# The first feed-forward product as seven half-size block products, in tiles of 512 tokens, with x' through DRAM

## Chip, cores, metric

One core of a Trainium2 chip. The metric is the time of one execution in microseconds (us) on the device. A run's profile has its own span (first to last instruction), some 2 us shorter than the time; sums over parts of a trace are sums of spans.

## The reference

Hash-masked attention (4 batches, 8 heads, 768 positions, head size 64), then a feed-forward block on the 3072 tokens. Only the second half is restructured:

```python
h = x @ w_in                                   # 3072 x 512 times 512 x 2048
sp = np.maximum(h, 0.0) + np.log1p(np.exp(-np.abs(h)))
g = h * erf(sp)
return (g @ w_out).astype(np.float32)          # times 2048 x 512
```

All of it is float32. The kernel computes the softplus with exp and log, and erf with a polynomial of three factors and a tanh.

## The kernel before

Tiles of 256 tokens. One unit is 512 rows of h for one tile; two units make an iteration, and there are 24 iterations. Of PSUM, the matmul accumulator, the kernel allots eight banks: three double ones for h and two single ones for the output.

```python
def hidden(u):                                   # first product of one unit
    ps = big("h_ps")[...]                        # one of three double banks
    for f in range(G):                           # 4
        for kc in range(NK):                     # 4
            nc.tensor.matmul(out=ps[:, f, :],    # 128 x 256
                lhsT=w_in_sb[:, kc, ...], rhs=xT[b][:, kc, t0 : t0 + T],
                start=(kc == 0), stop=(kc == NK - 1))
...
for p in range(NP + 3):
    if p < NP:
        hidden(2 * p); hidden(2 * p + 1)
    ...                                          # elementwise work of rounds p-1, p-2, p-3
    if check and 1 <= p:                         # input bounds, in the first 16 iterations
        for m in range(4 * p - 4, 4 * p):
            if m < 2 * B * H:
                extremes(m)                      # a DMA load, then a VectorE reduction
    if p >= 3:
        project(p - 3, 0); project(p - 3, 1)     # second product of round p-3
```

So the iterations 0 to 2 hold first products alone, and three rounds at the end hold second products alone. I call them start and tail, and the 21 in between full iterations.

## Time and profile before

| part of the trace before | from, to (us) | length |
|---|---|---|
| attention | 0 to 372.1 | 372.1 |
| start (iterations 0 to 2) | 372.1 to 414.8 | 42.7 |
| 21 full iterations | 414.8 to 993.6 | 578.8 |
| tail | 993.6 to 1043.4 | 49.8 |

The median time was 1046.42 us (three runs). The table is cut from the chain of work in order of time, whose lines the prediction shows.

### The profile page before, as it was taken

What the parts mean: (1) busy time and instruction counts of PE and PEld (TensorE: products, weight loads), DVE (VectorE), ACT (ScalarE), POOL (GpSimd) and SP (SyncE); (2) the same over time, 40 slices, a digit from 0 to 9 for tenths busy, and PEclk for the clock granted to TensorE, in tenths of its full rate; (3) what the DMA queues carried; (4) which work ended last, traced back from release to release, by engine and by line L of the source; (5) the groups of instructions that cost most, each with busy time, mean ns of one, the idle gap of its engine ahead of it and who ended that gap; (6) DMA issues with size and microseconds to landing.
All of it is one profiled execution on the core that took longest, in us unless ns stands there. A gap on an engine that the chain in (4) does not pass through costs nothing.

```text
span 1043.4 us, 11778 instructions
## 1 busy us (share of the span) xinstructions
PE 1028.2 (99%) x4482; PEld 603.4 (58%) x4482; DVE 797.4 (76%) x983; ACT 674.5 (65%) x770; POOL 16.2 (2%) x34
## 2 busy tenths in 40 slices
PE   7999999999999999999999999999999999999997
PEld 3444444444444478666666666666666666666643
DVE  4788888788888849988878787878786859494981
ACT  4666666565666637887777666666666667585880
POOL 0000000000000000000000000000000000000000
PEclk9999999999999999999999999999999999999999
DMA  8344445444443102011111101110111000000000
GB/s 197 87 102 122 113 134 138 106 102 103 123 123 96 58 17 61 30 35 63 40 41 31 36 30 52 31 51 30 51 31 35 1 21 0 21 1 11 10 21 24
DMA packets 55153, 61.98 MB, mean 59 GB/s; under 512 B 33552, under 2 KB 41744, under 8 KB 55088
## 3 DMA queue, kind: packets, MB, share of 16 engines
q1 hardware_dynamic: 50480, 45.41, 17.0%
q0 software_dynamic: 4320, 15.73, 4.7%
q8 instruction: 37, 0.61, 0.2%
q14 instruction: 28, 0.23, 0.1%
q10 hardware_dynamic: 288, 0.01, 0.0%
HBM read 54.63 MB, written 6.49 MB: 59 GB/s over the span
## 4 chain that ended last, share of the span: by engine, by line
PE 98%; DMA 1%; SPq 0%; DVE 0%; ACT 0%; issue 0%
PE h_ps L594 32%; PE o_ps L672 32%; PE st L319 15%; PE av L356 13%; PE bits L193 4%; PE z_ps L369 2%; DMA q<-in_qkT_dram 1%; SPq L178 0%; DVE ob L681 0%; DVE h L661 0%; SPq L183 0%; SPq L244 0%; ACT qb L209 0%; PE bound L748 0%
## 5 line engine op out<-in xcount | busy, mean ns | idle before, releaser
L594 PE MATMUL h_ps<-xT,w_in_sb 128*128 128x256 f32 x1536 | 335.4, 379 | 0.0
L672 PE MATMUL o_ps<-w_out_sb,h 128*128 128x512 f32 x768 | 333.3, 592 | 1.9 <-DVE h L661 1.9
L594 PEld LDWEIGHTS h_ps<-xT,w_in_sb 128*128 128x128 f32 x1536 | 291.6, 190 | 48.9 <-issue 10.0
L672 PEld LDWEIGHTS o_ps<-w_out_sb,h 128*128 128x128 f32 x768 | 145.8, 190 | 177.0 <-issue 172.7
L331 ACT ACTIVATE e<-st 128x768 f32<-128x768 f32 x192 | 141.1, 808 | 27.1 <-PE st L319 27.1
L356 PE MATMUL av<-e,v 128*64 128x385 f32 (+1 forms) x768 | 138.1, 495 | 0.0
L319 PE MATMUL st<-q,k 64*128 64x384 f32 x768 | 134.3, 482 | 0.0
L344 DVE TENSOR_TENSOR sum<-sum,e 128x768 f32<-128x768 f32 x128 | 121.5, 949 | 8.9
L653 DVE SCALAR_TENSOR_TENSOR s<-q,s 128x1024 f32<-128x1024 f32 x96 | 111.0, 1218 | 18.8 <-ACT q L652 18.8
L621 ACT ACTIVATE e<-e 128x1024 f32<-128x1024 f32 x48 | 50.0, 1049 | 96.2 <-DVE e L608 96.2
L652 ACT ACTIVATE q<-z,cq 128x1024 f32<-128x1024 f32 x96 | 102.5, 1137 | 1.3 <-DVE s L635 1.2
L356 PEld LDWEIGHTS av<-e,v 128*64 128x64 f32 x768 | 49.5, 136 | 80.6 <-issue 72.4
L607 ACT COPY h<-h_ps 128x1024 f32<-128x1024 f32 x48 | 47.9, 1000 | 72.9 <-PE h_ps L594 72.9
L319 PEld LDWEIGHTS st<-q,k 64*128 64x128 f32 x768 | 71.4, 187 | 37.8
L681 DVE COPY ob<-o_ps 128x512 f32<-128x512 f32 x24 | 16.4, 688 | 78.3 <-PE o_ps L672 78.3
L625 DVE TENSOR_TENSOR w<-e,w 128x1024 f32<-128x1024 f32 x48 | 58.8, 1225 | 1.7
L635 DVE SCALAR_TENSOR_TENSOR s<-s,w 128x1024 f32<-128x1024 f32 x48 | 58.8, 1225 | 1.6
L632 DVE SCALAR_TENSOR_TENSOR s<-h,s 128x1024 f32<-128x1024 f32 x48 | 58.5, 1218 | 0.0
L694 DVE TENSOR_REDUCE most<-t 128x1 f32<-128x384 f32 x64 | 33.1, 547 | 31.4 <-DMA t<-in_qkT_dram 31.3
L661 DVE TENSOR_TENSOR h<-h,s 128x1024 f32<-128x1024 f32 x48 | 56.4, 1217 | 0.0
L653 DVE SCALAR_TENSOR_TENSOR s<-z,s 128x1024 f32<-128x1024 f32 x48 | 56.4, 1216 | 0.0
L660 ACT ACTIVATE s<-s 128x1024 f32<-128x1024 f32 x48 | 49.6, 1054 | 9.4 <-DVE s L653 7.2
(58 smaller groups left out, 740.9 us busy)
## 6 DMA issues: line engine op xcount, KB each, us to landing
t<-in_qkT_dram SPq DMA_DIRECT2D x64, 192.0 KB
raw<-in_w_out_dram POOLq DMA_DIRECT2D x16, 512.0 KB, 4.2
raw<-in_w_in_dram POOLq DMA_DIRECT2D x14, 512.0 KB, 4.0
q<-in_qkT_dram SPq DMA_DIRECT2D x32, 192.0 KB
k<-in_qkT_dram SPq DMA_DIRECT2D x32, 192.0 KB
v<-in_v_dram SPq DMA_DIRECT2D x32, 192.0 KB
r<-rd SPq DMA_DIRECT2D x32, 192.0 KB
out_dram<-ob SPq DMA_DIRECT2D x24, 256.0 KB
```

Source lines behind the costliest of these rows:

```text
L319: nc.tensor.matmul(out=d["st"][c][:, ab, 0:HS], lhsT=d["k" + src][rows, keys], rhs=d["q" + src][rows, cols], start=(part == 0), stop=(part ...
L331: nc.scalar.activation(out=e[:, :, 0:HS], in_=st[:, :, 0:HS], func=AF.Exp, scale=scale)
L344: nc.vector.tensor_tensor(out=d[key], in0=d[key], in1=e, op=ALU.add)
L356: nc.tensor.matmul(out=d["av"][rows, 0:w], lhsT=d["v"][:, g * GC + c, rows], rhs=e[:, ab, 0:w], start=(g == 0 and c == 0), stop=(g == 1 an ...
L594: nc.tensor.matmul(out=ps[:, f, :], lhsT=w_in_sb[:, kc, (g * G + f) * P : (g * G + f + 1) * P], rhs=xT[b][:, kc, t0 : t0 + T], start=(kc = ...
L625: nc.vector.tensor_tensor(out=w, in0=e, in1=w, op=ALU.subtract)
L632: nc.vector.scalar_tensor_tensor(out=s, in0=h, scalar=0.0, in1=s, op0=ALU.max, op1=ALU.add)
L635: nc.vector.scalar_tensor_tensor(out=s, in0=s, scalar=S_MAX, in1=w, op0=ALU.min, op1=ALU.add)
L652: nc.scalar.activation(out=q, in_=z, func=AF.Square, bias=cq[:, j : j + 1])
L653: nc.vector.scalar_tensor_tensor(out=s, in0=q, scalar=r, in1=s, op0=ALU.add, op1=ALU.mult)
L661: nc.vector.tensor_tensor(out=d["h"], in0=d["h"], in1=s, op=ALU.mult)
L672: nc.tensor.matmul(out=ps, lhsT=st[t * NG + f // G]["h"][:, f % G, tt * P : (tt + 1) * P], rhs=w_out_sb[:, f, :], start=(f == 0), stop=(f ...
```

## The change

The intent is fewer matmuls. Strassen's scheme in its Winograd form does a product of 2 x 2 blocks with seven block products in place of eight, for extra sums of blocks. Weight sums are made once, during attention; sums of x once per tile; the sums of results come from accumulation in PSUM and three additions on VectorE. x' is the normalised output of attention, the x of the reference above.

```diff
-    T = 256
+    T = 512
+    w_sum = const.tile([P, 3, 2, FH], F32, name="w_sum")
+    xs = [dram.tile([JP, P, S], F32, ...) for b in range(B)]      # x' goes out and comes back
...
+            def product(p, name):
+                into, a, b, first, last = dict(
+                    P1=("X", a11, b11, True, False),
+                    P2=("Y", a12, b21, True, True),
+                    P3=("Z", s4, b22, False, True),
+                    P4=("X", a22, t4, False, True),
+                    P5=("Z", s1, t1, True, False),
+                    P6=("X", s2, t2, False, False),
+                    P7=("X", s3, t3, False, False),
+                )[name]                                            # 4 matmuls of 256 columns each
+            def read(p, q):                                        # ScalarE: X -> h
+                nc.scalar.copy(out=d["h"][:, :, q, :], in_=d["X"])
+            def complete(p, q, which):                             # VectorE: h += Y or Z
+                nc.vector.tensor_tensor(out=h, in0=d[which], in1=h, op=ALU.add)
+            def one_more(p, u):                                    # moved from VectorE
+                nc.scalar.activation(out=w, in_=st[p]["e", u], func=AF.Identity, bias=1.0)
...
+                    for name in ("P1", "P2", "P5"): product(p, name)
+                each(saturate, p - 3); each(gate, p - 3)
+                read(p, 0); complete(p, 0, "Y"); product(p, "P6")
+                project(p - 3, 0)
+                each(square, p - 2); each(factor, p - 2, 0)
+                each(absolute, p - 1); each(multiply, p - 2, 0)
+                read(p, 1); product(p, "P7")
+                project(p - 3, 1); project(p - 3, 2)
+                each(exponential, p - 1); each(one_more, p - 1)
+                presum_x(...); extremes(...) x4; check(...)
+                each(lost, p - 1)
+                read(p, 3); complete(p, 3, "Z"); product(p, "P4"); product(p, "P3")
+                each(logarithm, p - 1); each(softplus, p - 1); each(correct, p - 1)
+                each(factor, p - 2, 1); each(multiply, p - 2, 1)
+                each(factor, p - 2, 2); each(multiply, p - 2, 2)
+                read(p, 2); complete(p, 1, "Z")
+                project(p - 3, 3); store(...)
```

(Cut: the conditions for the first and last iterations, and all that only renames pools.) The order of these calls is the order in each engine's queue. X, Y and Z are one bank each, and four banks hold output, so the three double banks for h are gone.

## The prediction

> **What bounds the kernel now.** I read the page first: engine shares, then the chain that ended last, then the costliest groups.
>
> ```profile
> PE 1028.2 (99%) x4482; PEld 603.4 (58%) x4482; DVE 797.4 (76%) x983; ACT 674.5 (65%) x770; POOL 16.2 (2%) x34
> PE 98%; DMA 1%; SPq 0%; DVE 0%; ACT 0%; issue 0%
> L594 PE MATMUL h_ps<-xT,w_in_sb 128*128 128x256 f32 x1536 | 335.4, 379 | 0.0
> L672 PE MATMUL o_ps<-w_out_sb,h 128*128 128x512 f32 x768 | 333.3, 592 | 1.9 <-DVE h L661 1.9
> ```
>
> TensorE is busy all the time and is 98% of the chain: there is nothing but matmuls to save. Each f32 matmul of the program shows as two records (768 calls, 1536 records). The 379 ns is a latency with overlap; 335.4/1536 = 218 ns is the pitch.
>
> The chain in order of time gives the rhythm of the feed-forward part (columns: start us, us, what):
>
> ```profile
> 372.17 14.01 PE h_ps L594 x64
> 386.98 41.64 PE h_ps L594 x192
> 428.62 13.73 PE o_ps L672 x32
> 442.35 13.81 PE h_ps L594 x64
> ...
> 979.89 27.48 PE o_ps L672 x64
> 1009.28 27.75 PE o_ps L672 x64
> ```
>
> One iteration (24 of them) is 13.81 of first product plus 13.73 of second: 27.54 us. It starts with three iterations of first product alone, without a hole but for a 0.8 us divisor matmul: 372.2 to 414.8, 42.6 us. Then 21 full iterations to 993.6, then 49.8 us of tail: second products, a 1.9 us wait, the last copy and store.
>
> The elementwise groups of one shape, from the list by form, price what is added:
>
> ```profile
> L635 DVE SCALAR_TENSOR_TENSOR s<-s,w 128x1024 f32<-128x1024 f32 x48 | 58.8, 1225 | 1.6
> L608 DVE TENSOR_SCALAR e<-h 128x1024 int32<-128x1024 int32 x48 | 32.8, 684 | 27.2 <-ACT h L607 27.2
> L652 ACT ACTIVATE q<-z,cq 128x1024 f32<-128x1024 f32 x96 | 102.5, 1137 | 1.3 <-DVE s L635 1.2
> L694 DVE TENSOR_REDUCE most<-t 128x1 f32<-128x384 f32 x64 | 33.1, 547 | 31.4 <-DMA t<-in_qkT_dram 31.3
> L681 DVE COPY ob<-o_ps 128x512 f32<-128x512 f32 x24 | 16.4, 688 | 78.3 <-PE o_ps L672 78.3
> ```
>
> Last row but one: the check of extremes, four per iteration in the first 16, waits about 1.95 us each time for a DMA, because only two buffers serve four loads. That wait stays.
>
> [...] 13.81/64 = 216 ns per 256-column record, 13.73/32 = 429 ns per 512. So one matmul less saves its full time, and Strassen's smaller blocks lose nothing, since they keep 256 columns and 128 rows. [...] Trace: 1225 against 684 ns for the same 1024 elements. All block sums are two-source, so full price. [...] the trace shows two loads of 1283 ns per iteration, and I expect two. [...]
>
> **The change, part by part.**
> (1) Removed: per 512-token tile 112 block matmuls in place of 128, so 28 calls (56 records) an iteration in place of 64 records: 8 x 0.2158 = 1.73 us, a period of 12.08 + 13.73 = 25.81 us. In all 24 x 1.73 = 41.4 us, 4.0% of the time: the most it can give.
> (2) VectorE per iteration, from start to start when independent: 14 two-source operations of 1024 (gate 2, multiply 6, lost 2, softplus 2, correct 2) at 1.15 = 16.1; absolute 2 x 0.62 = 1.25; four new completions of 512 from PSUM at about 0.68 (the copy row's size) = 2.7; together 20.1. Block sums of x: four of 512 in four iterations, 0.65 each time. Output copies 4 x 0.69 in every fourth iteration. Extremes 4 x 0.52 + 1.95 wait = 4.0 in the first 16. The four copies share two buffers, so the third waits about 2 us for the store of the first. Mean in the first 16: 20.1 + 0.65 + 0.7 + 0.5 + 4.0 = 25.9, of which 2.4 is waiting; the period of TensorE is 25.81. It has no slack on the mean, but a store burst is 4.7 us late in one iteration and worked off in the three after it.
> (3) ScalarE: tanh, exp, log, square, one_more 10 x 1.0, factor 6 x 1.07, four reads of 512 at 0.58 (between 478 ns for 384 and 1000 for 1024), two loads 2.57: 21.3 us of 25.81.
> (4) The new waits. X, Y and Z are one bank each, so P6, P7, P4, P1 each wait for ScalarE to have read X, and P3, P5 for VectorE to have read Z. In a full iteration the projections of 3.43 us lie between them. I laid the three queues side by side: P7 is wanted at 10.3 us and read 1 ends at 7.6; P4 is wanted at 18.9 and read 3 ends at 12.8; P3 at 20.7 and the completion ends at 15.4; P5 of the next iteration at 29.3, completion at 25 to 28. After a store burst the gates end 6.3 us into the next iteration, the projection wants them at 6.9. So almost all is hidden; I put 0.2 us per iteration for near misses, 4 us. Once, in iteration 20, VectorE stands some 11 us at the check's matmul, which lies behind three projections: about 2.8 us of it reach TensorE.
> (5) The start. Iterations 0 to 2 have no projection to lie between reads. Iteration 0: 12.1 of work, divisor 0.8, then waits for the divisor's copy ahead of read 0, for read 1 and read 3: 15.7. Iteration 1: exp and one_more (4 us) stand in ScalarE's queue between read 1 and read 3, so P4 waits 3 us: 16.3. Iteration 2: square, factor, a table load, exp, one_more before read 3, then load, log and four factors before read 2, which P1 of iteration 3 waits for: about 19.3 of ScalarE work plus waits for VectorE, 23. Sum 55.0 against 42.6 before: +12.4 us, where the saving would have been 5.2.
> (6) The tail. Three more rounds of elementwise work follow, at the pace of ScalarE and VectorE, with only 13.73 of second product each. Following tanh, gate, exp, log, softplus, correct, multiply, gates of round 22 end some 20.6 us after the last first product, where before they ended at 15.6; TensorE idles 6 us there, then runs 27.5 to the end, copy and store 6.4: 54.5, [...] against 49.8: +6.
> (7) Weight sums (8 x 1.15) and x' through DRAM lie in the attention part, where TensorE bounds and VectorE has about 4 us free in 25: hidden, +1 for the handover at the end.
>
> Sum: 1046.4 - 21 x 1.73 (36.3) + 12.4 + 6 + 4 + 2.8 + 1 = 1036 us.
>
> **The rivals.**
> A: fully hidden. The reads slip in everywhere and start and tail cost nothing more; only then does the whole 41 us arrive: 1005 us. For it: TensorE's 98% of the chain, and queues with 10% free. Against it: the start has nothing to lie between reads, and the old kernel had three double banks of PSUM for it. With half of the start hidden and no tail loss it is about 1022.
> B: VectorE becomes the bound in the first 16 iterations. By (2) its mean is 25.9; if completions from PSUM cost 0.2 us more each, or each interleaved wait adds 1.5 us, the period there is 27.5 and that gain is gone: 1036 + 13 x 1.7 = 1058. For it: the DMA wait of the extremes, the store burst with two buffers. Against it: much of the 25.9 is waiting that can overlap other waits.
> C: the handshake on single banks. Each of six dependences costs TensorE a semaphore and 0.6 us even in full iterations: 21 x 2 = 42 us, so 1075. Against it: 3.4 to 7 us of other products stand before each dependent one.
>
> **Range and chances.** The sure part is 36 us of steady gain; the losses at the ends come from queue order and are sure in sign, with some 5 us of error each. B in part is the likelier error upwards, A in part downwards. So 1036, with 1022 to 1049 for 8 in 10. Faster by over 2% means under 1025.5: 0.2. Slower by over 2% needs B and C together: 0.05.
>
> **What would show it.** 1344 first-product records in place of 1536, at the same pitch, busy near 294 us. In the chain, mid-run, iterations of 25.8 to 26.0 us and matmuls nearly without pieces of ACT or DVE. Three first iterations of about 55 us with TensorE waiting for the reads (copies out of X) by 3 to 5 us at a time. A tail near 55 us with one hole of some 6 us. VectorE busy above 90% in iterations 3 to 16, about 80% after. Wrong if iterations in the first 16 are 27 us or more (B), if waits for reads or completions recur in every iteration (C), if the three first iterations take under 48 us (A), if table loads exceed two an iteration, or if attention ends more than 3 us later than before.

Where the recorded text is cut (marked), no trace of this case showed what it said. The figures left in the paragraph that opens with a cut are from the old kernel's trace: 216 and 429 ns a record, 1225 ns for a two-source operation (L635) against 684 for a one-source one (L608), table loads of 1283 ns. The recorded sum comes to 1036.3, given as 1036. The +6 of the tail in it held a term for a lower clock after the hole, which is cut; the terms that stand give 54.5 - 49.8 = +4.7 there, and a sum of 1035.0.

## More of the kernel before

The busy time by stretch (columns: stretch, length, then busy us and count for TensorE, weight loads, VectorE, ScalarE, GpSimd, then granted clock, which is TensorE's share of full speed by the trace, DMA share, GB/s) says what room the other engines had:

```profile
414.80:993.60 578.80, 578.80 (x2020) 383.02 (x2019) 452.06 (x479) 407.94 (x394) 0.00 (x0) 1.00 0.09 29
993.60:1043.40 49.80, 41.50 (x97) 17.84 (x95) 24.27 (x23) 20.18 (x20) 0.00 (x0) 0.96 0.06 23
```

In the full iterations TensorE has no hole at all; VectorE is busy 78% and ScalarE 70%.

## The result

The changed kernel is correct and takes 1032.76 us (1031.75 to 1035.13, 4 runs) against 1046.34 (1045.20 to 1048.01, 4 runs). The ratio is 0.9872, 95% interval 0.9851 to 0.9894: 1.3% faster, within 2%. Ratios in this document are the mean time of one kernel's runs over that of the other's in the same rounds, so not quite the ratio of the medians quoted.

The profiled run is the slowest of the four (span 1033.3). First its engine shares and its chain of work that ended last:

```profile
PE 997.1 (96%) x4290; PEld 569.3 (55%) x4290; DVE 828.1 (80%) x1039; ACT 728.0 (70%) x866; POOL 16.2 (2%) x34
PE 88%; DVE 4%; ACT 3%; DMA 2%; issue 1%; SPq 1%; DVEq 0%; ACTq 0%
```

The chain is no longer TensorE alone: 7% of it is VectorE and ScalarE. Where they stand in it shows in the chain in order of time (start us, us, what). A full iteration:

```profile
457.19 1.73 PE X L699 x8
...
464.10 3.43 PE o_ps L811 x8
...
469.26 6.87 PE o_ps L811 x16
...
479.58 3.43 PE o_ps L811 x8
483.01 1.73 PE X L699 x8
```

From X to X it takes 483.01 - 457.19 = 25.82 us, and every piece between is a matmul. The busy time by stretch, for iterations 1 and 2 and for two parts of the full ones:

```profile
391.55:408.96 17.41, 14.46 (x57) 11.39 (x56) 11.38 (x17) 9.20 (x11) 0.00 (x0) 0.90 0.24 70
408.96:430.33 21.37, 14.20 (x58) 11.32 (x56) 18.43 (x22) 18.75 (x21) 0.00 (x0) 0.92 0.23 74
430.33:767.00 336.67, 336.16 (x1145) 217.51 (x1146) 291.42 (x329) 273.22 (x288) 0.00 (x0) 1.00 0.16 50
767.00:973.00 206.00, 203.64 (x698) 131.76 (x697) 161.64 (x173) 166.44 (x176) 0.00 (x0) 1.00 0.05 17
```

TensorE fills 336.16 of 336.67 us in the first part, with VectorE at 87%. In iterations 1 and 2 it has holes and a granted clock of 0.90 and 0.92. TensorE in order of time shows them (in brackets the idle time before and what ended it):

```profile
403.56 2.62 PE L699 MATMUL X<-ts,w_in_sb 128*128 128x256 f32 x8 [2.27 <-ACT h L713]
406.12 3.00 PE L699 MATMUL Z<-x,w_sum 128*128 128x256 f32 x8
408.96 1.89 PE L699 MATMUL X<-x,w_in_sb 128*128 128x256 f32 x8
...
422.38 3.40 PE L699 MATMUL X<-ts,w_in_sb 128*128 128x256 f32 x8 [3.68 <-ACT h L713]
...
430.33 1.99 PE L699 MATMUL X<-x,w_in_sb 128*128 128x256 f32 x8 [2.81 <-ACT h L713]
```

P4 of iterations 1 and 2 and P1 of iteration 3 wait for reads of X (L713), and after two of the holes the products take 2.62 to 3.40 us in place of 1.9. Why the read was late is in ScalarE's queue of iteration 1:

```profile
399.14 2.00 ACT L735 ACTIVATE e<-e 128x1024 f32<-128x1024 f32 x2
401.05 1.99 ACT L739 ACTIVATE w<-e 128x1024 f32<-128x1024 f32 x2
402.94 0.57 ACT L713 COPY h<-X 128x512 f32<-128x512 f32 x1
```

Exp and one_more, 4 us, stand ahead of read 3. The tail, TensorE again:

```profile
977.06 14.00 PE L811 MATMUL o_ps<-w_out_sb,h 128*128 128x512 f32 x32 [0.23 <-DVE h L799]
996.97 30.28 PE L811 MATMUL o_ps<-w_out_sb,h 128*128 128x512 f32 x64 [5.90 <-DVE h L799]
```

A hole of 5.90 us for the gates (L799), then 64 records in 30.28 us where the old kernel took 27.75.

| part | before | after | difference | predicted |
|---|---|---|---|---|
| attention and handover | 372.1 | 375.35 | +3.2 | +1 |
| start | 42.7 | 55.0 | +12.3 | +12.4 |
| full iterations | 578.8 | 546.5 | -32.3 | -29.5 (= -36.3 + 4 + 2.8) |
| tail | 49.8 | 56.5 | +6.7 | +6 |
| sum of spans | 1043.4 | 1033.3 | -10.1 | -10.1 |

That this sum agrees to the tenth is luck: the other runs of the changed kernel have spans of 1030.0 to 1031.1. In this trace 2.3 us of the attention's +3.2 arise in the first 17 us, where the first matmuls waited longer for their loads (2.15 us in place of 0.93 before the third set of bits). In the twelve traces of this kernel and its variants below, whose attention part is the same, the feed-forward part begins anywhere between 372.2 and 376.9 us, with a median of 373.3, so about 2 us of that row are scatter.

### The profile page after: what moved, and what is told of

It is laid out like the page before. It is cut to its first block, busy times and chain, and to the rows that moved or that the text cites. A ratio compares the mean times of both kernels' runs of the same rounds, so it can differ in the third digit from the quotient of the medians.

```text
span 1033.3 us, 11568 instructions
## 1 busy us (share of the span) xinstructions
PE 997.1 (96%) x4290; PEld 569.3 (55%) x4290; DVE 828.1 (80%) x1039; ACT 728.0 (70%) x866; POOL 16.2 (2%) x34
## 4 chain that ended last, share of the span: by engine, by line
PE 88%; DVE 4%; ACT 3%; DMA 2%; issue 1%; SPq 1%; DVEq 0%; ACTq 0%
PE o_ps L811 30%; PE X L699 15%; PE st L367 14%; PE av L404 12%; PE Z L699 8%; PE bits L235 4%; PE Y L699 4%; PE z_ps L420 2%; DVE s L784 1%; DVE s L760 1%; DMA q<-in_qkT_dram 1%; DMA x<-xs 1%; DVE s L754 1%; ACT e L735 1%; ACT w L739 1%
## 5 line engine op out<-in xcount | busy, mean ns | idle before, releaser
L811 PE MATMUL o_ps<-w_out_sb,h 128*128 128x512 f32 x768 | 342.9, 596 | 6.1 <-DVE h L799 6.1
L713 ACT COPY h<-X 128x512 f32<-128x512 f32 x96 | 56.0, 584 | 86.4 <-PE X L699 86.4
L699 PE MATMUL X<-x,w_in_sb 128*128 128x256 f32 x384 | 91.2, 380 | 5.4 <-ACT h L713 4.8
L699 PEld LDWEIGHTS X<-x,w_in_sb 128*128 128x128 f32 x384 | 72.5, 190 | 34.8 <-issue 19.1
L744 DVE SCALAR_TENSOR_TENSOR w<-w,e 128x1024 f32<-128x1024 f32 x48 | 56.5, 1217 | 11.1 <-ACT w L739 11.1
L438 ACT COPY x<-av 128x384 f32<-128x384 f32 x32 | 15.3, 479 | 60.2 <-PE av L404 60.2
L784 DVE SCALAR_TENSOR_TENSOR s<-z,s 128x1024 f32<-128x1024 f32 x48 | 56.5, 1220 | 0.0
L760 DVE SCALAR_TENSOR_TENSOR s<-s,w 128x1024 f32<-128x1024 f32 x48 | 56.5, 1219 | 0.0
L799 DVE TENSOR_TENSOR h<-h,s 128x1024 f32<-128x1024 f32 x48 | 56.5, 1220 | 0.0
L699 PE MATMUL X<-ts,w_in_sb 128*128 128x256 f32 x192 | 47.8, 394 | 6.6 <-ACT h L713 6.6
```

The source lines that it names most:

```text
L699: nc.tensor.matmul(out=d[into][:, u, :], lhsT=a[:, kc, f : f + P], rhs=b[:, kc, :], start=(first and u == 0 and kc == 0), stop=(last and u ...
L744: nc.vector.scalar_tensor_tensor(out=w, in0=w, scalar=-1.0, in1=st[p]["e", u], op0=ALU.add, op1=ALU.subtract)
L760: nc.vector.scalar_tensor_tensor(out=s, in0=s, scalar=S_MAX, in1=st[p].pop(("w", u)), op0=ALU.min, op1=ALU.subtract,)
L784: nc.vector.scalar_tensor_tensor(out=s, in0=st[p]["q", u], scalar=ERF_Q[j][1], in1=s, op0=ALU.add, op1=ALU.mult,)
L799: nc.vector.tensor_tensor(out=h, in0=h, in1=st[p].pop(("s", u)), op=ALU.mult)
L811: nc.tensor.matmul(out=o_live[tt], lhsT=st[p]["h"][:, u, 2 * fh + half, sub * P : (sub + 1) * P], rhs=w_out_sb[:, fh * NF // 2 + 2 * c + u ...
```

## The experiments

Theory: a product left out is worth its whole time because TensorE sets the period of the full iterations; the gain is partly given back at both ends, where no projection lies between the dependent products, so that the queues of ScalarE and VectorE set the pace. Rivals: VectorE bounds the full iterations (B), or the handshake on single banks does (C). Times are medians; each run's ratio is to the old kernel in the same rounds.

### e1: an eighth product

```diff
-                    for name in ("P1", "P2", "P5"):
+                    for name in ("P1", "P2", "P2", "P5"):
```

> P2 is computed twice in every iteration, with the same result, so each iteration has 64 records of first product as the old kernel had, in the new kernel's order. Theory (TensorE bounds every full iteration, a product left out saves its whole time): 21 full iterations at 25.82 + 1.73 = 27.55 us, so +36 us there, and up to +5 us in the first three: 1032.8 + 36 to 41 = 1069 to 1074 us. Rivals (VectorE or the waits on X and Z already set the period, so the eighth product fits into holes): under +20 us, below 1053.

Measured: 1080.66 us, ratio 1.0332 (1.0293 to 1.0371). That is 48 us more than the changed kernel, more than I had expected. The chain of its trace in order of time:

```profile
463.13 1.74 PE Y L699 x8
464.87 0.04 issue
464.92 1.99 PE Y L699 x8
```

The second P2 is a new tile in the same bank, and its weight loads wait for the first one's matmuls (17 such waits between 440 and 930 us, 0.5 us at most). Its period from X to X is 489.28 - 461.40 = 27.88 us, 2.06 more than 25.82: 1.73 for the matmuls, 0.33 for this wait, which the experiment brought in. 24 x 2.06 = 49 us. What follows: the 1.73 us arrive in full (TensorE is busy 439.08 of the 440 us between 460 and 900 us), so nothing else set the period, and the rivals (under 20 us) fall.

### e2 and e5: how far VectorE was from being the bound

Each iteration gets three more two-source operations, `h = max(h, h)` over 1024 elements, ahead of `lost`. e5 also splits the extremes:

```diff
+                if 1 <= p <= NP:
+                    extra(p - 1, 3)
                 each(lost, p - 1)
# e5 only:
-                    for m in range(4 * p - 4, 4 * p):        # four extremes in one place
+                    for m in range(4 * p - 4, 4 * p - 2):    # two here, two after correct
```

> Three more two-source VectorE operations of 1024 elements per iteration (h = max(h, h), result unchanged), 3 x 1.15 = 3.45 us. Theory (what counts is busy time plus the 1.95 us wait for the extremes' loads): VectorE had 291.4 us busy over 13.04 iterations from 430 to 767 us, 22.35 each; with the extras 25.8, with the wait 27.75, so the 14 full iterations with extremes take about 27.7 in place of 25.82, +27 us; the 7 later ones (20.3 + 3.45 = 23.7) stay at 25.82; start and tail about +7: about 1067 us. Rival (only busy time counts, 13.4% of 25.82 = 3.46 us were free): full iterations stay at 25.82 and the time is about 1040.

> As e2_vector3, but two of the four extremes are moved behind the softplus correction, so that the two buffers are free when their loads start and VectorE need not wait the 1.95 us. Theory (the wait was part of VectorE's period): the 14 iterations come down to 25.8 to 26.3 us, the time to about 1040 to 1047. Rival (the wait lay beside other waits and did not count): as e2_vector3, within 5 us.

Measured: e2 1073.01 us, ratio 1.0253 (1.0223 to 1.0283); e5 1041.20 us, ratio 0.9951 (0.9920 to 0.9982). Eight iterations of e2 and of e5, busy time by stretch:

```profile
552.99:776.19 223.20, 210.93 (x705) 133.84 (x705) 204.18 (x225) 165.21 (x177) 0.00 (x0) 0.99 0.15 48
```

```profile
563.82:772.09 208.27, 207.10 (x705) 133.60 (x705) 203.26 (x225) 166.97 (x177) 0.00 (x0) 1.00 0.16 51
```

Both have VectorE busy for 204 and 203 us, so for 25.5 an iteration, under the 25.82 that TensorE needs. Yet e2's period is 223.20/8 = 27.90 and e5's 26.03. The waits of e2 between 434 and 800 us (who waits, for what: total, times, longest) name the difference:

```profile
DVE most L838 <- DMA t<-in_qkT_dram: 25.7, 13, 2.1
...
PE Z L699 <- DVE h L718: 16.2, 12, 2.9
```

VectorE waits 2 us per iteration for the third load of the extremes, which needs one of two buffers, and TensorE waits for VectorE to have read Z. In e5 that wait doesn't appear at all, and TensorE waits for Z 3.4 us in all. In the eight iterations of e2 shown above VectorE waits for nothing but DMAs: 15.8 us for the extremes' loads and 3.1 for stores, which with the 204.18 busy make up the 223.20. What follows: a wait in VectorE's queue counts like busy time once the queue has no other place to lose it. Rival B was near, but not true of the changed kernel: between 430.33 and 767 us VectorE is busy 22.35 us an iteration (291.42 over 336.67/25.82 = 13.04 iterations) and waits 2.4 for DMAs (26.4 for loads and 4.7 for stores in all), which leaves some 1.1 us. e2 came 6 us above what was expected; its start is the larger part (73.1 us from the first X to the first projection, 62.8 in the changed kernel, where 7 us had been put for start and tail together).

### e3: projections no longer between the products

```diff
                     product(p, "P6")
-                if p >= 3:
-                    project(p - 3, 0)
...                                            # likewise 1 and 2; all four after P3
```

> The seven products run back to back and the four projections after them. Theory (single banks are harmless only because projections stand between): P7 waits some 0.7 us for read 1; P4 waits for read 3, which stands behind exp and one_more, about 3 us; P3 some 1 us for the completion; so about 30 us an iteration, +4 x 21 = 85 us, 1090 to 1140 in all. Rival (a read costs TensorE only a semaphore, order matters little): under +10 us.

Measured: 1131.75 us, ratio 1.0817 (1.0776 to 1.0857), 99 us more than the changed kernel. TensorE in order of time, one iteration:

```profile
469.77 1.99 PE L699 MATMUL X<-x,w_in_sb 128*128 128x256 f32 x8 [0.68 <-ACT h L713]
474.03 1.99 PE L699 MATMUL X<-ts,w_in_sb 128*128 128x256 f32 x8 [2.27 <-ACT h L713]
476.82 1.99 PE L699 MATMUL Z<-x,w_sum 128*128 128x256 f32 x8 [0.79 <-DVE h L718]
```

The two waits for X, 0.68 and 2.27, are those of iteration 1 in the start, and both come back in nearly every iteration (41 waits for X between 430 and 1060 us); the one for Z, 0.79 here, comes in two of three (14 waits). The sizes are near those expected (0.7, 3 and 1). So rival C is real without the interleaving and absent with it: single banks are harmless in the changed kernel because 3.4 to 7 us of other matmuls stand ahead of each dependent product.

### e4: idle matmuls in the hole of the tail

```diff
                     project(p - 3, 3)
+                    if p == NP:
+                        idle_matmuls(12)      # 128 x 256, into the unused bank X
```

> Twelve idle matmuls of 256 columns (5.2 us) go into the unused bank X in TensorE's hole of 5.9 us in the tail. Theory (the hole lowers the granted clock, and the last 64 records take 30.3 us in place of 27.5 for that alone): they take 27.5 again, the time falls by 2 to 3 us. Rival (they are slower because their operands or banks are contended in the tail): no change, or +0.5.

Measured: 1029.69 us, ratio 0.9846 (0.9834 to 0.9859), some 3 us faster by the medians. The two intervals overlap a little, so the trace has to show it. TensorE in order of time:

```profile
992.26 5.34 PE L805 MATMUL X<-x,w_in_sb 128*128 128x256 f32 x24
998.33 27.73 PE L823 MATMUL o_ps<-w_out_sb,h 128*128 128x512 f32 x64 [0.72 <-DVE h L799]
```

The last 64 records take 27.73 us in place of 30.28, and the tail is 53.8 us long in place of 56.5. In the changed kernel the granted clock of those records is 0.91; in the old one they take 27.75 us at 1.00. They work on the same operands, so it was the clock after the hole, as the theory had it.

### e6, e9, e10: the start

e6 shortens ScalarE's queue, e9 takes the extremes out of VectorE's queue in the start, e10 does both.

```diff
# e6: iteration 1
+                if p == 1:
+                    each(exponential, p - 1)          # ahead of read 1
                 read(p, 1); product(p, "P7")
# e6: one_more of rounds 0 and 1
-                nc.scalar.activation(out=w, in_=e, func=AF.Identity, bias=1.0)
+                nc.vector.tensor_scalar(out=w, in0=e, scalar1=1.0, scalar2=None, op0=ALU.add)
# e9: extremes from iteration 3 on
-                    for m in range(4 * p - 4, 4 * p):
+                    for m in range(4 * p - 12, 4 * p - 8):
```

> In iteration 1 exp stands before read 1 in ScalarE's queue, and in iterations 1 and 2 one_more runs on VectorE. Theory (the three first iterations are long because reads of X stand behind elementwise work in ScalarE's queue): P4 of iteration 1 waits under 1 us in place of 2.3, P4 of iteration 2 about 2 us less, the first projection starts 4 to 6 us earlier: 1027 to 1029. Rival (VectorE's chain of round 0 sets the start, ScalarE's order does not): within 1.5 us of before.

Measured: 1036.87 us, ratio 0.9904 (0.9891 to 0.9917): slower than the changed kernel by some 4 us. My expectation was wrong, and so was its rival. TensorE's waits for X shrank as expected (P4 of iteration 1 waits 0.68, of iteration 2 1.79), but in their place stand waits for Z:

```profile
405.61 2.93 PE L699 MATMUL Z<-x,w_sum 128*128 128x256 f32 x8 [2.85 <-DVE h L718]
...
428.31 3.78 PE L699 MATMUL Z<-x,w_sum 128*128 128x256 f32 x8 [5.65 <-DVE h L718]
```

VectorE's one_more has to wait for exp (0.52 and 0.25 us in iteration 1), and everything behind it in VectorE's queue waits with it: the block sum, four extremes with their DMA wait (2.00), `lost`, and the completion that frees Z. Before, the extremes ran while ScalarE did exp and one_more. That explanation is new, so I tested it:

> The new kernel with one edit: the extremes start two iterations later, so VectorE has none of them, and none of their waits, in the iterations that fill the pipeline. Theory now (in the start ScalarE's order holds the new kernel, and VectorE's extremes lie beside ScalarE's exp and one_more): within 1.5 us of the new kernel, 1031 to 1034. Rival (the extremes on VectorE hold the start of the new kernel too): 3 us or more faster.

> The edit of e6_start and that of e9_later together. e6 made ScalarE's chain shorter but waited for Z: 2.85 us before P3 of iteration 1 and 5.65 before P3 of iteration 2, for completions behind extremes. Theory (the start is held by whichever of the two queues is longer, so both have to be shortened): those two waits fall under 0.5 and about 2 us, the first projection starts 3 to 4 us earlier than in the new kernel: 1028 to 1030, some 7 us below e6. Rival (one_more on VectorE is itself what made e6 slower): no better than e9_later.

Measured: e9 1031.07 us, ratio 0.9855 (0.9840 to 0.9869); e10 1030.04 us, ratio 0.9835 (0.9819 to 0.9850). The start is best read from the traces, from the first X to the first projection: 62.77 us in the changed kernel (375.35 to 438.12), 67.40 in e6, 62.50 in e9, 59.41 in e10. The extremes alone change nothing in the start (e9; that its median is 1.7 us lower is within the scatter, since the intervals overlap); with ScalarE's queue shortened they were worth 67.40 - 59.41 = 8.0 us. In e10 the wait for Z in iteration 1 is gone and the one in iteration 2 is

```profile
419.42 1.99 PE L699 MATMUL Z<-x,w_sum 128*128 128x256 f32 x8 [1.74 <-DVE h L718]
```

So the start is held by whichever queue is longer, and shortening one alone pays nothing, or costs. By the medians e10 gained only 2.7 us on the changed kernel, a little under what I had expected. Against e9, run in the same rounds, all five times of e10 are lower, so one_more on VectorE is not itself what made e6 slower.

### e7, e8, e11: the tail, and all together

e7 orders the tail by age: all of round 22 up to its gates ahead of the logarithm of round 23, with one_more of round 23 on VectorE.

```diff
+            each(square, 22); each(factor, 22, 0); each(absolute, 23); each(multiply, 22, 0)
+            each(exponential, 23)
+            each(factor, 22, 1) ... each(multiply, 22, 2)
+            each(saturate, 22); each(lost, 23); each(gate, 22)      # then the projections of 22
+            each(logarithm, 23); each(softplus, 23) ... each(gate, 23)
```

> After the last first product the oldest round goes first: all of the polynomial and gate of round 22 before the logarithm of round 23, and one_more of round 23 on VectorE. Theory (the tail is long for queue order, a chain of about 20 us from gate 21 to gate 22): the gates of round 22 end before the projections of round 21 do, the hole of 5.9 us goes, a hole of some 3.5 us comes before the last projections: -4 to -5 us, about 1028. Rival (the tail is bound by the whole work of ScalarE, about 30 us): the hole only moves, within 1.5 us.

Measured: 1030.84 us, ratio 0.9854 (0.9840 to 0.9868), some 2 us faster by the medians, with overlapping intervals, where 4 to 5 were expected; its tail is 54.3 us in place of 56.5. TensorE in the tail:

```profile
990.47 14.00 PE L816 MATMUL o_ps<-w_out_sb,h 128*128 128x512 f32 x32 [1.53 <-DVE h L804]
1007.16 15.70 PE L816 MATMUL o_ps<-w_out_sb,h 128*128 128x512 f32 x32 [2.69 <-DVE h L804]
```

The hole of 5.90 became two of 1.53 and 2.69, 4.2 in all. Most of it only moved, which is the rival's part: this order alone doesn't remove it. That the amount of elementwise work is the bound isn't shown, though: in this tail ScalarE idles 3.63 us for VectorE, and VectorE 2.22 us for ScalarE. And after the 2.69 us the records were slower: 32 took 15.70 us in place of 14.00.

> e6 and e7 together, six idle matmuls in the hole before the last projections, and the check's matmul of iteration 20 moved ahead of that iteration's projections, which takes away VectorE's wait of 11.4 us there and TensorE's two waits of 1.56 and 0.80. If the parts add: -5 (start) -5 (tail) -2.4 (check) -1 (clock) = about 1020, 2.5% below the old kernel. If start and tail do not add, 1025 or more.

Measured: 1030.49 us, ratio 0.9848 (0.9835 to 0.9861). The parts did not add, since it carries e6's start (67.41 us to the first projection). The -1 for the clock in the expectation was an estimate; with the idle matmuls the last 32 records take 14.00 us, where e7 has 15.70. Its tail is 52.8 us against 56.5, and the check's two waits, 1.56 and 0.80 us, are gone. That asked for the same with e9's edit:

> e8_all with the extremes two iterations later (and the check one later, still ahead of the projections). If the gains add: new kernel 1032.8, start -3.5, tail -3.7 (as the tail of e8 measured), check -2.4: 1022 to 1025, some 7 us below e8_all. If over 1027, the gain of the start is taken back in the full iterations.

Measured: 1022.87 us (1021.12 to 1025.76, 5 runs), ratio 0.9776 (0.9756 to 0.9795): 2.2% faster than the old kernel and some 10 us faster than the changed one, with correct results. The gains of start, tail and check add here. It is the fastest of the kernels run. In its start the granted clock stayed at 1.00, which by itself gained nothing: TensorE is busy 27.80 us between 397 and 434 us where e10, with the same work there, has 29.44 at a granted clock of 0.95, but both reach the first projection 59.41 us after the first X. e11 waits for Z (P5 of iteration 3) where e10 was still at work:

```profile
429.05 1.99 PE L699 MATMUL Z<-ts,w_sum 128*128 128x256 f32 x8 [1.75 <-DVE h L718]
```

Its start (first X to P1 of iteration 3) is 50.4 us (373.20 to 423.58), so 7.7 us of the old kernel's lead there remain.

## Why the prediction was right

The prediction was right by time (1036 against 1032.76, range 1022 to 1049) and by its order of sizes, and the mechanism that it named is the one that the runs show. Step by step:

1. **The saving per iteration.** Predicted 25.81 us; the chain shows 25.82, and e1 gives the 1.73 back, apart from the wait that e1 brought in itself. What carries the step is the proportion measured here, 216 ns a record of 256 columns and 429 of 512. The 1344 records came, but they are busy 306.8 us and not 294: the trace counts the end of each group, and a group of eight shows 1.89 us though the next starts after 1.73; the lower granted clock of iterations 1 and 2 (0.90 and 0.92) adds to it.
2. **VectorE.** Predicted mean 25.9 with 2.4 of waiting, busy above 90%; measured 22.35 busy, 87%, and 2.4 of waiting. The step miscounted: there are three completions an iteration and not four (72 of L718 in 24 iterations; the fourth quarter, read 2, needs none), and they start 0.60 us apart and not 0.68, so 1.8 us in place of 2.7, most of the error. The large operations start 1.135 us apart in place of 1.15. So VectorE had some 1.1 us of slack where the prediction saw none. The rest of the step held: the DMA wait of the extremes stayed (28.3 us in 16 waits between 434 and 800 us), the third copy waited for a store (longest 1.6 us, 2 predicted), and e2 with e5 shows that such waits count like busy time.
3. **ScalarE.** Predicted 21.3 us an iteration; 273.22/13.04 = 21.0. Table loads stayed at two per iteration (24 and 23 of 1283 ns, as in the old kernel), so the new Identity brought none.
4. **New waits in full iterations.** The queues as laid out hold: in the iteration from 457.03 us, read 3 ends after 12.9 us (12.8 predicted) and the completion that frees Z after 14.7 (15.4), while P4 starts after 18.9 (18.9). But a term was mis-sized: I put 4 us for near misses, and between the wait of iteration 3 (0.51 us, which makes that iteration 0.9 us longer) and the check there is no hole in TensorE. These 3 us are the largest part of the error in the median. The check's step was right: VectorE waits 11.39 us for the matmul behind three projections, and TensorE then 1.56 and 0.80 us, with which that iteration is 3.2 us longer (2.8 predicted).
5. **The start.** 55.0 predicted, 55.0 measured, though its parts differ: 16.2, 17.4 and 21.4 us for 15.7, 16.3 and 23. So the sum is in part luck. Iteration 0 was longer though its clock was 1.00: TensorE was busy 13.78 us there, where 12.9 had been put for products and divisor. In iteration 1 it was busy 14.46 us at a clock of 0.90, which I had left out. The holes were 2.3 to 3.7 us and smaller ones of 0.7, not 3 to 5. That ScalarE's queue sets the start was half of the truth: e6 shows VectorE's close behind.
6. **The tail.** +6 predicted, +6.7 measured, with the hole of 5.9 (6 predicted) and 2.5 us for the last 64 records at a granted clock of 0.91.
7. **Attention.** Hidden as predicted; the handover shows 0.58 us before the first X and 0.20 before a matmul of the attention. By the letter one sign of being wrong came true: attention ended 3.2 us later than before, and the limit was 3. But over the twelve traces the median is 1.2 us later (1 predicted), so I take the rest for scatter of the opening, which one trace of the old kernel can't settle.

Rival A did not come: start and tail are 19 us longer than before, where fully hidden the start would have been 5 us shorter. B is 1.1 us per iteration away, C is held off by the interleaving. Two sums of the rivals, with 0.2 and 0.6 us that were supposed and not measured, were careless: four completions at 0.2 us more give 26.7 us an iteration and not 27.5 (B), and six dependences at 0.6 us are 3.6 us an iteration and not 2 (C).

## What to carry to other kernels

A saving on the bounding engine arrived in full here where the pipeline was full (25.82 us an iteration for 25.81 predicted), so take the number of full rounds times the saving, and then price the fill and the drain by themselves: there the work that hides the new handshakes is missing. Add up waits with busy time when you ask how near a second engine is to becoming the bound. When two queues feed the same wait, shortening one may bring nothing (e9) or cost time (e6), so try both together (e10), and look for loads or checks in the start that could as well come later.

## What else the traces show

- Holes of TensorE of the same length were followed by slower records in one run and not in another. After 2.27 us P4 took 2.62 and P3 3.00 in the changed kernel (granted clock 0.68 from 403.56 to 408.96 us), and after 2.69 us 32 records took 15.70 in place of 14.00 (e7). The same hole of 2.27 us cost nothing in e7 and e9 (P4 1.99, P3 at most 1.99), and one of 2.22 us before P1 of iteration 3 cost in e10 (3.19) and not in e11 (1.99). Why one hole acts differently from run to run is not shown.
- The trace has two records per call of a float32 matmul in the feed-forward part, 216 ns each at 256 columns and 429 at 512, so 432 and 858 ns a call.
- All 49 table loads of the changed kernel take 1283 ns. In one switch a read ends at 469.89 us, the load starts at 469.90 and the logarithm at 471.20, so the switch took 1.31 us.
- An addition on VectorE with one operand in PSUM costs no more here than with both in SBUF: 686 ns (Z, L718) and 689 (Y, L718) against 687 (L200), for 512 elements.
